# Queries by kv in one float32r pass a head, with the parts stacked in the rows, and statistics begun a chunk ahead

## The chip, the cores and the metric

The kernel runs on one core of one Trainium2 chip. The metric is the device time of one execution in microseconds. A core has TensorE (PE; its weight loads are listed as PEld), VectorE (DVE), ScalarE (ACT), GpSimd (POOL) and SyncE (SP), which here issues all DMAs. The engines work side by side, each through its own list of instructions in order, and wait for one another by semaphores.

## The reference

Linear attention over 8 batches, 8 heads, 576 tokens of 64 numbers, and behind it a gated feed-forward layer on the 4608 tokens of 512 numbers (`w_a` and `w_b` are 512 x 1536, `w_out` is 1536 x 512), all in float32:

```python
q_s = np.exp(q - max(q, axis=-1));  q_s = q_s / (sum(q_s, axis=-1) + 1e-09)
k_s = np.exp(k - max(k, axis=2));   k_s = k_s / (sum(k_s, axis=2) + 1e-09)
kv  = einsum('bhsd,bhse->bhde', k_s, v)
x   = einsum('bhsd,bhde->bhse', q_s, kv)      # 4608 x 512 after a transposition
a, b = x @ w_a, x @ w_b
out  = (a * b) @ w_out
```

## The kernel before, in words

**Number format.** A float32 number is kept as two float32r parts, hi and lo, and a product of two float32 matrices is three matmul passes: hi by hi, hi by lo, lo by hi. `split` makes the parts: a cast for hi (ACT, L341, or DVE), a subtraction for lo (DVE, L344).

**Chunks and loops.** The 4608 tokens are worked in nine chunks (0 to 8) of T = 512. The loop over `c` from 1 to 8 multiplies chunk `c` with both gate matrices, one of six pairs of 128 features of `w_a` and `w_b` after the other, and meanwhile prepares the attention result of chunk `c + 1`. A pair is computed by a scheme with seven products of half size instead of eight, from sums of blocks: `kx` = A11 B11, `ky` = S2 T2, `ka` = S3 T3, `kp` = S1 T1, then `kx` += A12 B21, `kp` += S4 B22 and `ka` += A22 T4. Each is 12 matmuls of 256 columns (`product`, L835) into one of three PSUM banks (k0 for `kx`, k1 for `ky` and then `kp`, k2 for `ka`), with weights `ws` that SP loads from DRAM (L475) and operands `xo` made of the chunk's `xf`. Between the products ACT copies `kx` to `u2` (L1443), DVE adds `ky`, `ka` and `kp` to it (L1444 to L1474), multiplies the halves and splits the gate's product to `gh` and `gl` (L341, L344). `run_pending` multiplies these by `w_out` into the four banks `po` (L864). So `kx` can be written a second time only when ACT has copied it, and `ky` of a pair only when DVE has read the `kp` that was in its bank.

**Preparing a chunk.** Three calls of `attend()` in each pair run a list of steps that `attention_tasks(c + 1)` has written, 18 calls in a loop. The steps for a batch that begins in the chunk are the softmax of k and kv = kT v for two heads at a time (`kv_two`, `pk`, L582), stored as a weight pair `kvh`, `kvl` of 128 x 128 with zeros outside the heads' own blocks. For the queries there are, for each of four head pairs `g`:

- `q_load` and `q_stats`: the queries by tokens; the negative maximum on DVE (L672), then eight exponentials of 128x64 on ACT with a summing output (L675), and small DVE operations. Behind the fourth pair `q_stats_out` transposes all statistics on TensorE (`pst`), copies them and writes them to DRAM as `dq` (L690).
- `q_rows`: four DMAs read `dq` back, spread over 64 rows each, as `mr` (L716: the negative maximum in `rows[0]`, the reciprocal sum in `rows[1]`); `q_turned`: the queries by features, `qtt`.
- `q_exp`: DVE adds `rows[0]`, ACT takes the exponential, `split` makes `qhl`.
- `x_product`: `px` = kv by q, three passes in the spare bank "at", in two pieces where a batch ends inside the chunk (L761); DVE multiplies by `rows[1]` into `xf` (L960).

**What sets the order.** The list of steps gives the call in which a step is issued. Tile's scheduler then orders each engine's instructions by its model of the times, buffers rotate through a few tiles each, and a table (`ORDER`) fixes the order of the first chunks' work. SP issues DMAs in that order, and one that waits holds up those behind it.

Of the kernel before, what the change touches and what calls it, by code (L numbers as in the profile page):

```python
# [255 lines left out]
def linear_attention_then_gated_ffn(  # L256
# [40 lines left out]
    TT = T // P  # L297
    NCH = NT // T
    LATE = NCH - qt_late.shape[0]

    const = ctx.enter_context(tc.tile_pool(name="const", bufs=1))
    sb = ctx.enter_context(tc.tile_pool(name="sb", bufs=2))
# [35 lines left out]
    def split(hi, lo, src, hi_engine="act"):  # L338

        if hi_engine == "act":  # L340
            nc.scalar.copy(out=hi, in_=src)  # L341
        else:
            nc.vector.tensor_copy(out=hi, in_=src)
        return nc.vector.tensor_tensor(out=lo, in0=src, in1=hi.bitcast(F32), op=ALU.subtract)  # L344
# [270 lines left out]
    def kv_two(b, g, kts, vts, tag):  # L615

        pk = ps.tile([P, 2, D + 1], F32, name="pk", tag=tag)
        for n in range(2):
            kv_sums(kts[n], vts[n], tag, pk[:, n])
        den = sb.tile([P, 2], F32, name="den2")  # L620
        nc.vector.tensor_scalar_add(den, pk[:, :, D], EPS)
        nc.vector.reciprocal(out=den, in_=den)
        kv = sb.tile([P, 2, P], F32, name="kv2", bufs=1)
# [6 lines left out]
        split(*kv_home(b, g), kv, "dve")  # L630


    wholes = sb.tile([P, 2, NP, P], F32, name="wholes", tag="mr", bufs=2)
# [5 lines left out]
    def kv_split_whole(b, g):  # L639
        kv_split(b, g, whole.pop((b, g)))  # L640
# [54 lines left out]
    def roomy(c):  # L695
        return c > LATE

# [23 lines left out]
    def q_exp(c, qt, rows):  # L721
        nc.vector.tensor_tensor(out=qt, in0=qt, in1=rows[0], op=ALU.add)
# [19 lines left out]
    def x_whole(c, g, qw, tag):  # L742

        t0 = c * T
        b0, b1 = t0 // S, (t0 + T - 1) // S
        n0 = min(T, (b0 + 1) * S - t0)
        px = ps.tile([P, T], F32, name="px", tag=tag)
        for b, s in ((b0, slice(0, n0)), (b1, slice(n0, T)))[:b1 - b0 + 1]:
            nc.tensor.matmul(px[:, s], whole[b, g], qw[:, s], start=True, stop=True)  # L749
        return px  # L750

    def x_product(c, g, qhl, tag="at"):
        qh, ql = qhl
# [161 lines left out]
                steps += [(), ()] * (g > 0) + [(s0, s1, s2)]  # L915
        return steps

    def attention_tasks(c):
# [12 lines left out]
        stats, last, turned, rows = [], [], [], []  # L931
        every = {}
        for g in range(NP):
            box = {}

            def a0(g=g, box=box):
                if g == 0:
                    every["st"] = sb.tile([P, NP, 2, 2, TT], F32, name="st", bufs=1)
                box["q"] = q_load(c, g)

            def a1(g=g, box=box):
                q_stats(box["q"], every["st"][:, g])
                if g == NP - 1:
                    every["dq"] = q_stats_out(c, every["st"])

            stats.append((a0, a1))
# [11 lines left out]
            def b2(g=g, box=box):  # L958
                px = x_product(c, g, box["e"])
                nc.vector.tensor_tensor(out=xfs[c][:, g], in0=px, in1=box["r"][1], op=ALU.mult)  # L960

            turned.append(t0)
            rows.append(r0)
            last.append((b1, b2) if roomy(c) else (lambda t0=t0, r0=r0: (t0(), r0()), b1, b2))
        stats, steps = pipeline(stats), pipeline(steps)
        seq = []
        for i in range(max(len(stats), len(steps))):
            seq.append((stats[i] if i < len(stats) else []) + (steps[i] if i < len(steps) else []))
        last = pipeline(last)
        if c > 3:  # L970
            begin = 3 * NI - 3 - len(last) - 2
# [419 lines left out]
    last = None  # L1391
    for c in range(1, NCH):
        more = c + 1 < NCH
        attend = Spread(attention_tasks(c + 1) if more else [], 3 * NI - 3 - (1 if c == 1 else 0))
        po = None
        x, xo = xo, {}
        pairs = list(range(NI))[::-1 if c % 2 else 1]
        for n, i in enumerate(pairs):
            def part(name):
                return named(f"{name}.{(c - 1) * NI + n}") if c < 5 else nullcontext()  # L1400
# [51 lines left out]
            if not end:  # L1452
                with part("proj"):
                    run_pending()
            with part("attend"):
                attend(c > 2 and last)
            kp = ps.tile([P, 2, H], F32, name="kp", tag="k1")
            multiply(kp, S1, T1, True)
            multiply(kx, A12, B21, False)
            with part("pair"):  # L1460
                nc.vector.tensor_tensor(out=cc[:, 3], in0=kp, in1=u3, op=ALU.add)  # L1461
                nc.scalar.copy(out=cc[:, 0, 0], in_=kx[:, 0])  # L1462
# [4 lines left out]
                    run_pending()  # L1467
            if po is None:
                po = [ps.tile([P, DM], F32, name=f"po{t}") for t in range(TT)]
            with part("attend"):  # L1470
                attend(c > 2 and last)
            multiply(kp, S4, B22, False)
# [65 lines left out]
```

## Time and profile before

| | us |
|---|---|
| median of 3 runs | 935.83 (935.6 to 938.75) |
| the profiled execution | 935.81 |
| its span | 934.0 |
| TensorE busy | 924.7 |
| VectorE busy | 618.0 |
| ScalarE busy | 394.0 |
| GpSimd busy | 107.9 |

The times come from one core; the profiled execution is one of the program's, recorded by the hardware profiler, and 1.81 us of it lie outside the span. Matmuls are pipelined: a group's busy time overlaps the next group's start, so what matmuls cost is read from one start to the next.

### The profile page before, as it was taken

The numbers are of one execution on the slowest core, as the hardware profiler recorded it, in microseconds if no ns is written. First come the engines' busy times: TensorE is split into PE (matmuls) and PEld (weight loads), VectorE is DVE, ScalarE is ACT, GpSimd is POOL, SyncE is SP. The second block draws the span as 40 slices with busy tenths as digits, with TensorE's granted clock in tenths as the row PEclk, the third lists the DMA queues.
The fourth block names the chain that finished last, engine by engine and source line by source line (L and its number), as shares of the span: only waits on it lengthen the run. The fifth ranks groups of instructions, "written<-read, shape, count | busy, mean of one in ns | idle before, by whom it ended". The sixth has DMA issues, their size and how long they took to land.

```text
span 934.0 us, 17535 instructions
## 1 busy us (share of the span) xinstructions
PE 924.7 (99%) x6565; PEld 835.2 (89%) x6565; DVE 618.0 (66%) x1218; ACT 394.0 (42%) x1094; POOL 107.9 (12%) x88
## 2 busy tenths in 40 slices
PE   8999999999999999999999999999999999999998
PEld 6677789999988999999999999999999999999997
DVE  7998898788854677467656574666657454753433
ACT  8988774435521345133613271324424352322111
POOL 1654434330000000000100010000000000000000
PEclk9999999999999999999999999999999999999999
DMA  9989889989788879983989289945997389627761
GB/s 349 349 308 367 333 321 337 330 310 285 266 305 291 259 270 345 283 330 110 337 255 380 94 302 297 361 169 198 331 320 247 102 293 308 219 96 270 248 224 47
DMA packets 88947, 253.27 MB, mean 271 GB/s; under 512 B 10720, under 2 KB 11296, under 8 KB 88864
## 3 DMA queue, kind: packets, MB, share of 16 engines
q1 hardware_dynamic: 88864, 252.16, 78.5%
q8 instruction: 52, 0.85, 0.4%
q14 instruction: 31, 0.25, 0.1%
HBM read 213.09 MB, written 36.93 MB: 268 GB/s over the span
## 4 chain that ended last, share of the span: by engine, by line
PE 95%; DVE 2%; DMA 1%; ACT 0%; POOL 0%; issue 0%; SPq 0%; DVEq 0%; POOLq 0%
PE po L864 31%; PE kx L835 14%; PE kp L835 14%; PE ka L835 14%; PE pt L805 7%; PE ky L835 7%; PE px L761 2%; PE pk L582 2%; PE po L850 1%; PE px L749 1%; DMA kt_first<-in_kt 1%; DVE xo L344 0%; POOL mx L512 0%; DVE kt L544 0%; DVE mc L1128 0%
## 5 line engine op out<-in xcount | busy, mean ns | idle before, releaser
L864 PE MATMUL po<-wo_w,gh 128*128 128x512 f32 x840 | 264.5, 396 | 0.0
L835 PE MATMUL kx<-xo,ws 128*128 128x256 f32 x1152 | 184.7, 282 | 0.3 <-DVE cc L1463 0.2
L835 PE MATMUL ka<-xo,ws 128*128 128x256 f32 x1152 | 177.7, 282 | 0.7 <-DVE u L1447 0.4
L835 PE MATMUL kp<-xo,ws 128*128 128x256 f32 x1152 | 174.8, 283 | 0.5 <-DVE cc L1461 0.5
L864 PEld LDWEIGHTS po<-wo_w,gh 128*128 128x128 f32 x840 | 151.3, 188 | 25.1 <-ACT gh L341 0.5
L835 PEld LDWEIGHTS kx<-xo,ws 128*128 128x128 f32 x1152 | 160.7, 189 | 6.7 <-DVE cc L1463 0.7
L835 PEld LDWEIGHTS ka<-xo,ws 128*128 128x128 f32 x1152 | 157.9, 189 | 6.7 <-issue 0.6
L835 PEld LDWEIGHTS kp<-xo,ws 128*128 128x128 f32 x1152 | 155.7, 189 | 5.8 <-DVE cc L1461 0.8
L864 PE MATMUL po<-wo_w,gl 128*128 128x512 f32 x420 | 153.0, 396 | 0.0
L341 ACT CAST gh<-cc 128x512 fp32r<-128x512 f32 x96 | 58.6, 620 | 168.8 <-DVE cc L1475 145.4
L1462 ACT COPY cc<-kx 128x256 f32<-128x256 f32 x48 | 17.8, 372 | 177.6 <-PE kx L835 170.4
L864 PEld LDWEIGHTS po<-wo_w,gl 128*128 128x128 f32 x420 | 78.0, 188 | 15.7 <-DVE gl L344 0.4
L1474 DVE TENSOR_TENSOR cc<-kp,u 128x512 f32<-128x512 f32 x48 | 33.1, 690 | 86.0 <-PE kp L835 85.9
L805 PE MATMUL pt<-xo,ws 128*128 128x512 f32 x288 | 87.0, 418 | 0.0
L835 PE MATMUL ky<-xo,ws 128*128 128x256 f32 x576 | 86.6, 281 | 0.0
L675 ACT ACTIVATE qt<-qt,st 128x64 f32<-128x64 f32 x224 | 75.3, 340 | 19.6 <-DVE st L672 18.7
L835 PEld LDWEIGHTS ky<-xo,ws 128*128 128x128 f32 x576 | 76.8, 189 | 1.1
L344 DVE TENSOR_TENSOR gl<-cc,gh 128x512 fp32r<-128x512 f32 x96 | 67.1, 704 | 12.9 <-ACT gh L341 12.8
L1461 DVE TENSOR_TENSOR cc<-kp,u 128x512 f32<-128x512 f32 x48 | 33.2, 691 | 62.7 <-PE kp L835 62.2
L805 PEld LDWEIGHTS pt<-xo,ws 128*128 128x128 f32 x288 | 52.9, 188 | 17.3 <-issue 4.2
L512 POOL PARTITION_ALL_REDUCE mx<-m x20 | 18.1, 910 | 433.0 <-DVE m L523 433.0
L1443 ACT COPY u<-kx 128x512 f32<-128x512 f32 x48 | 28.0, 583 | 51.5 <-PE kx L835 48.0
(150 smaller groups left out, 1117.3 us busy)
## 6 DMA issues: line engine op xcount, KB each, us to landing
ws<-dw SPq DMA_DIRECT2D x260, 512.0 KB, 6.0
dw<-ws SPq DMA_DIRECT2D x42, 512.0 KB, 6.6
mr<-dq SPq DMA_DIRECT2D x112, 128.0 KB, 6.0
raw<-in_w_ab SPq DMA_DIRECT2D x24, 512.0 KB, 7.8
out<-ot SPq DMA_DIRECT2D x36, 256.0 KB, 4.7
vt<-in_v SPq DMA_DIRECT2D x28, 325.0 KB, 6.1
qt<-in_q SPq DMA_DIRECT2D x32, 256.0 KB, 5.1
kt<-in_k SPq DMA_DIRECT2D x24, 320.0 KB, 5.3
```

Of the source, the lines that this page charges most:

```text
L341: nc.scalar.copy(out=hi, in_=src)
L344: return nc.vector.tensor_tensor(out=lo, in0=src, in1=hi.bitcast(F32), op=ALU.subtract)
L512: nc.gpsimd.partition_all_reduce(out_ap=mx, in_ap=kv_max(kt), channels=P, reduce_op=bass_isa.ReduceOp.max,)
L582: nc.tensor.matmul(pk[h * D:(h + 1) * D], kt[:, j, h], vt[:, j, h], start=(j == 0), stop=(j == J - 1),)
L675: nc.scalar.activation(out=qt[:, j, h], in_=qt[:, j, h], func=AF.Exp, bias=st[:, h, 0, j:j + 1], accum_out=st[:, h, 1, j:j + 1],)
L761: nc.tensor.matmul(px[:, s], w, m[:, s], start=(i == 0), stop=(i == 2))
L805: nc.tensor.matmul(pt, w[:, wp], x[g][:, xp], start=(g == 0 and i == 0), stop=(g == NP - 1 and i == 2),)
L835: ins = nc.tensor.matmul(pt[:, n], w[:, n, wp, c], x[:, xp, c], start=(first and n == 0 and i == 0), stop=(i == 5), skip_group_check=True,)
L864: ins = nc.tensor.matmul(po[t], a[:, ts], wo[f][:, w], start=(f == ends[0] and i == 0), stop=(f == ends[1] and i == 2),)
L1443: nc.scalar.copy(out=u2, in_=kx)
L1461: nc.vector.tensor_tensor(out=cc[:, 3], in0=kp, in1=u3, op=ALU.add)
L1474: nc.vector.tensor_tensor(out=cc[:, 1], in0=kp, in1=u2, op=ALU.add)
```

## The change

From chunk 5 on (`TALL = 5`, the sixth) a product of queries by kv is made head by head. The 64 rows of a head's queries that were in half of the rows of a tile are put there twice: the hi parts in the head's own half of one tile, the lo parts in the other half. The weight pair for a head has hi over hi in the columns of its own head, and lo over zeros in the other 64 columns. One pass of 128 rows then gives hi·hi + hi·lo in the head's own 64 output rows and lo·hi in the other 64. ACT copies the second half to the head's own rows of `rows[0]`, DVE adds the two halves, and one multiplication by `rows[1]` ends a head pair, as before. The two heads use two banks: "at", and whichever of k0 and k1 is free at this call. For it,

- `kv_tall` writes the weights of a batch with 64-row casts on DVE and ACT, a subtraction on DVE and a fill with zeros on POOL, and `kv_again` does it a second time for batch 4, on which chunk 5 begins;
- `q_exp` splits the two heads apart, with two casts and two subtractions of 64 rows;
- in loops with `c + 1 >= TALL` the product A12 B21 into `kx` is moved ahead of S1 T1 into `kp`, so that a bank is free;
- the queries' statistics of chunk `c + 2` are begun in loop `c`, for c = 3 to 6: loads at calls 11, 12, 16 and 17, the statistics of the first two head pairs at 12 and 14, of the other two at calls 0 and 1 of the next loop, and the rows, exponentials and products at fixed calls (products at 5, 7, 10 and 13; before at 10 to 14).

TensorE has 6166 matmuls in its list instead of 6194: 56 instead of 84 for `px` of chunks 5 to 8. DVE has 1282 instructions instead of 1220, ACT 888 instead of 824, POOL 110 instead of 94 and SP 672 DMAs as before.

```diff
+    def kv_tall(b, g, heads):
+        q = g // 2
+        w = [sb.tile([P, 2, P], F32R, name=f"kvt{x}{q}", tag=f"kv{x}{q}") for x in "hl"]
+        for n in (2 * q, 2 * q + 1):
+            kvs[b, n] = tuple(t[:, n % 2] for t in w)
+        for h, (hi, lo) in enumerate(heads):
+            me, it = own(h), own(1 - h)
+            nc.vector.tensor_copy(out=w[h][me, :, me], in_=hi)
+            nc.scalar.copy(out=w[h][it, :, me], in_=hi)
...
+            nc.gpsimd.memset(w[h][it, :, it].bitcast(F32), 0.0)
...
     def q_exp(c, qt, rows):
         nc.vector.tensor_tensor(out=qt, in0=qt, in1=rows[0], op=ALU.add)
         nc.scalar.activation(out=qt, in_=qt, func=AF.Exp)
+        if c >= TALL:
+            hl = sb.tile([P, 2, T], F32R, name="qhl", tag="mr", bufs=2)
+            for h in range(2):
+                split(hl[own(h), h], hl[own(1 - h), h], qt[own(h)])
+            return hl
...
+    def x_tall(c, g, hl, rows, xf):
...
+        for h, tag in enumerate((at["spare"], "at")):
+            px = ps.tile([P, T], F32, name=f"px{h}", tag=tag)
+            for s in (slice(0, edge), slice(edge, T))[:1 + (edge < T)]:
+                nc.tensor.matmul(
+                    px[:, s], kvs[(t0 + s.start) // S, g][h], hl[:, h, s], start=True, stop=True
+                )
+            me = own(h)
+            nc.scalar.copy(out=rows[0][me], in_=px[own(1 - h)])
+            nc.vector.tensor_tensor(out=xf[me], in0=px[me], in1=rows[0][me], op=ALU.add)
+        nc.vector.tensor_tensor(out=xf, in0=xf, in1=rows[1], op=ALU.mult)
...
+                for g, n in enumerate((5, 7, 10, 13)):
+                    exp, mul = every["last"][g]
+                    seq[max(n - 3, 3)] = seq[max(n - 3, 3)] + [rows[g], turned[g]]
+                    seq[n - 1] = seq[n - 1] + [exp]
+                    seq[n] = [mul] + seq[n]
...
+        if TALL <= c + 2 < NCH:
+            every, stats = stats_steps(c + 2)
+            todo, calls = todo + [[] for _ in range(len(todo), calls + 3)], calls + 3
+            for g, n in enumerate((11, 12, 16, 17)):
+                todo[n] = todo[n] + [stats[g][0]]
+            for g, n in enumerate((12, 14)):
+                todo[n] = todo[n] + [stats[g][1]]
+            ahead[c + 2] = every, [[s[1]] for s in stats[2:]]
...
+            if c + 1 >= TALL:
+                multiply(kx, A12, B21, False)
             kp = ps.tile([P, 2, H], F32, name="kp", tag="k1")
             multiply(kp, S1, T1, True)
-            multiply(kx, A12, B21, False)
+            if c + 1 < TALL:
+                multiply(kx, A12, B21, False)
```

How this moves instructions is shown at two places. The first is ScalarE in loop 6, in the fifth of the six pairs, where chunk 7 is prepared. A row has the line, the operation, what it writes and reads, and the size; `gh` is a gate's cast, `qtt` the exponential of the queries, `qhl` their hi part, `u` the copy of `kx`. Before:

```order
L723 ACTIVATE qtt<-qtt 128x512
L341 CAST qhl<-qtt 128x512
L341 CAST gh_8445<-cc 128x512
L341 CAST gh_8465<-cc 128x512
L1443 COPY u_8473<-kx 128x512
```

and now, where the rows of `qt,st` are the statistics of chunk 8:

```order
L342 CAST gh_8594<-cc 128x512
L758 ACTIVATE qtt<-qtt 128x512
L710 ACTIVATE qt,st<-qt,st 128x64
L342 CAST qhl<-qtt 64x512 x2
L710 ACTIVATE qt,st<-qt,st 128x64 x7
L1536 COPY u_8602<-kx 128x512
L342 CAST gh_8574<-cc 128x512
```

Eight instructions of the statistics and two casts of 64 rows have come between the exponential of the queries and the copy of `kx`. TensorE has in the same pair now:

```order
L890 MATMUL ka<-xo,ws 128x256 x3
L890 MATMUL kx<-xo,ws 128x256 x12
L890 MATMUL kp<-xo,ws 128x256 x12
L890 MATMUL ka<-xo,ws 128x256 x12
L890 MATMUL ky<-xo,ws 128x256 x12
L799 MATMUL px_8686<-qhl,kvtl_6992 128x448
L799 MATMUL px_8686<-qhl,kvtl_8198 128x64
L890 MATMUL kx<-xo,ws 128x256 x12
```

The first row ends the pair before. The second `kx` has moved ahead of `po` and `kp`, and one head's pass, in two pieces, stands right ahead of it.

The other place is the queue of SP, from the statistics' way to DRAM on: `dq` is written, and `mr` are the rows read back, `ws` weights, `kt` and `vt` the keys and values of a batch. Before, in loop 6:

```order
L690 DMA dq_7987<-sst 64x128
L475 DMA ws<-dw_740 128x1024
L475 DMA ws<-dw_856 128x1024
L716 DMA mr_8231<-dq_7987 64x512
L716 DMA mr_8232<-dq_7987 64x512
L716 DMA mr_8231<-dq_7987 64x512
L716 DMA mr_8232<-dq_7987 64x512
L716 DMA mr_8285<-dq_7987 64x512
```

and now:

```order
L725 DMA dq_7854<-sst 64x128
L476 DMA ws<-dw_621 128x1024
L476 DMA ws<-dw_586 128x1024
L751 DMA mr_8017<-dq_7854 64x512
L501 DMA kt<-in_k 128x640
L507 DMA vt<-in_v 128x650
L501 DMA kt<-in_k 128x640
L507 DMA vt<-in_v 128x650
L751 DMA mr_8018<-dq_7854 64x512
L751 DMA mr_8017<-dq_7854 64x512
L751 DMA mr_8018<-dq_7854 64x512
L751 DMA mr_8107<-dq_7854 64x512
```

Three more `mr` and two `ws` follow in both. The rows come at another time of the loop, and four loads of keys and values now lie between them, behind the one that waits for `dq`.

More of the change, by code (lines that the diff above doesn't have):

```diff
@@ L299, in linear_attention_then_gated_ffn @@
     LATE = NCH - qt_late.shape[0]
+    TALL = 5
     const = ctx.enter_context(tc.tile_pool(name="const", bufs=1))
@@ L622, in kv_two @@
         nc.vector.reciprocal(out=den, in_=den)
+        if b * S >= TALL * T:
+            kv = sb.tile([P, 2, P], F32, name="kv2", bufs=1)[:, :, 0:D]
+            nc.vector.tensor_tensor(
+                out=kv, in0=pk[:, :, 0:D], in1=den.unsqueeze(2).broadcast_to([P, 2, D]), op=ALU.mult,
+            )
+            kv_tall(b, g, [(kv[own(h)], None) for h in range(2)])
+            return
         kv = sb.tile([P, 2, P], F32, name="kv2", bufs=1)
@@ L630, in kv_two, with own, kv_again @@
         split(*kv_home(b, g), kv, "dve")
+    def own(h):
+        return slice(h * D, (h + 1) * D)
+    def kv_tall(b, g, heads):
[7 more added lines that the diff above has]
+            nc.scalar.copy(out=w[h][it, :, me], in_=hi)
+            if lo is None:
+                nc.vector.tensor_tensor(
+                    out=w[h][me, :, it], in0=hi, in1=w[h][me, :, me].bitcast(F32), op=ALU.subtract
+                )
+            else:
+                nc.vector.tensor_copy(out=w[h][me, :, it], in_=lo)
+            nc.gpsimd.memset(w[h][it, :, it].bitcast(F32), 0.0)
+    def kv_again(b):
+        for g in range(0, NP, 2):
+            kvh, kvl = kv_parts[b, g // 2]
+            kv_tall(b, g, [[x.bitcast(F32)[own(h), :, own(h)] for x in (kvh, kvl)] for h in range(2)])
     wholes = sb.tile([P, 2, NP, P], F32, name="wholes", tag="mr", bufs=2)
@@ L916, in key_steps, with stats_steps, a0, a1 @@
         return steps
+    ahead = {}
+    def stats_steps(c):
+        every, stats = {}, []
+        for g in range(NP):
+            box = {}
+            def a0(g=g, box=box):
+                if g == 0:
+                    every["st"] = sb.tile([P, NP, 2, 2, TT], F32, name="st", bufs=1)
+                box["q"] = q_load(c, g)
+            def a1(g=g, box=box):
+                q_stats(box["q"], every["st"][:, g])
+                if g == NP - 1:
+                    every["dq"] = q_stats_out(c, every["st"])
+            stats.append((a0, a1))
+        return every, stats
     def attention_tasks(c):
@@ L930, in attention_tasks @@
                 ))
-        stats, last, turned, rows = [], [], [], []
-        every = {}
-        for g in range(NP):
[L934 to L946, printed above, removed]
+        if c == TALL and c * T % S:
+            steps = [(lambda: kv_again(c * T // S),)] + steps
+        last, turned, rows = [], [], []
+        if c in ahead:
+            every, stats = ahead[c][0], []
+        else:
+            every, stats = stats_steps(c)
+        for g in range(NP):
             box = {}
@@ L958, in b2 @@
             def b2(g=g, box=box):
+                if c >= TALL:
+                    x_tall(c, g, box["e"], box["r"], xfs[c][:, g])
+                    return
                 px = x_product(c, g, box["e"])
@@ L968, in attention_tasks @@
             seq.append((stats[i] if i < len(stats) else []) + (steps[i] if i < len(steps) else []))
+        every["last"] = last
         last = pipeline(last)
         if c > 3:
+            if c >= TALL:
+                seq = [[] for _ in range(3 * NI - 3)]
+                for n, now in enumerate(ahead[c][1]):
+                    seq[n] = seq[n] + now
+                for n, now in enumerate(steps):
+                    seq[n] = seq[n] + now
+                for g, n in enumerate((5, 7, 10, 13)):
[3 more added lines that the diff above has]
+                    seq[n] = [mul] + seq[n]
+                return seq
             begin = 3 * NI - 3 - len(last) - 2
@@ L1393, in linear_attention_then_gated_ffn @@
         more = c + 1 < NCH
-        attend = Spread(attention_tasks(c + 1) if more else [], 3 * NI - 3 - (1 if c == 1 else 0))
+        todo, calls = attention_tasks(c + 1) if more else [], 3 * NI - 3 - (1 if c == 1 else 0)
+        if TALL <= c + 2 < NCH:
[6 more added lines that the diff above has]
+            ahead[c + 2] = every, [[s[1]] for s in stats[2:]]
+        attend = Spread(todo, calls)
         po = None
@@ L1469, in linear_attention_then_gated_ffn @@
                 po = [ps.tile([P, DM], F32, name=f"po{t}") for t in range(TT)]
+            at["spare"] = "k0"
             with part("attend"):
```

4 lines of the change are left out of this document (added).

## The prediction, made before the changed kernel was run

> **What bounds the kernel now.** I read the page first: the profiled execution took 935.81 us, 934.0 of them span, so 1.81 us lie around the span, and the sum below is made against 935.81. The median shown, 935.83, is the same within 0.02.
>
> ```profile
> span 934.0 us, 17535 instructions
> PE 924.7 (99%) x6565; PEld 835.2 (89%) x6565; DVE 618.0 (66%) x1218; ACT 394.0 (42%) x1094; POOL 107.9 (12%) x88
> PE 95%; DVE 2%; DMA 1%; ACT 0%; POOL 0%; issue 0%; SPq 0%; DVEq 0%; POOLq 0%
> ```
>
> TensorE is busy 99% of the span and 95% of the chain that ended last. That is an average, so I cut the time by stages next. A row of the windows view has the stretch and its length, then busy time (and instructions) of PE, PE's weight loads, DVE, ACT and POOL, the granted clock, the DMA share and GB/s.
>
> ```profile
> 300.00:500.00 200.00, 200.00 (x1512) 185.28 (x1511) 128.80 (x261) 73.17 (x222) 7.52 (x8) 1.00 0.83 276
> 700.00:900.00 200.00, 200.00 (x1384) 186.04 (x1383) 106.45 (x194) 56.37 (x149) 0.00 (x0) 1.00 0.67 223
> ```
>
> From 300 to 900 us, where all that is changed takes place (the first TensorE instruction that differs stands at about 380 us), TensorE never waits: 200.00 of 200.00 us at clock 1.00. So here a matmul less is time won at once, and any wait that TensorE gets is time lost at once. In the first of the two stretches DVE is busy 128.80/200 = 64%, ACT 37%, the DMA 83%: room on average, which does not say that they are never late.
>
> **What the change takes away.** In the products of queries by kv of chunks 5 to 8, three passes become two of the same width, one a head. The timeline of TensorE shows one product of each of the four chunks. Where the product lies between others, its cost is from its start to the next row's start.
>
> ```profile
> 501.92 0.46 PE L761 MATMUL px<-qhl,kvh 128*128 128x320 f32 x2
> 502.22 0.31 PE L761 MATMUL px<-qhl,kvl 128*128 128x320 f32 x1
> ...
> 502.68 0.54 PE L835 MATMUL kx<-xo,ws 128*128 128x256 f32 x3
> ```
>
> ```profile
> 597.46 0.52 PE L761 MATMUL px<-qhl,kvh 128*128 128x384 f32 x2
> ...
> 598.27 1.64 PE L835 MATMUL kp<-xo,ws 128*128 128x256 f32 x12
> ```
>
> ```profile
> 697.04 0.56 PE L761 MATMUL px<-qhl,kvh 128*128 128x448 f32 x2
> ...
> 697.89 1.68 PE L835 MATMUL kp<-xo,ws 128*128 128x256 f32 x12
> 699.41 0.76 PE L835 MATMUL ka<-xo,ws 128*128 128x256 f32 x5
> ```
>
> ```profile
> 798.02 0.62 PE L761 MATMUL px<-qhl,kvh 128*128 128x512 f32 x2
> 798.48 0.39 PE L761 MATMUL px<-qhl,kvl 128*128 128x512 f32 x1
> 798.71 1.23 PE L835 MATMUL kx<-xo,ws 128*128 128x256 f32 x9
> ```
>
> Chunk 5: 0.76 us, chunk 6: 0.81, chunk 7: 0.85, chunk 8: 0.69. A third of each is 0.25, 0.27, 0.28 and 0.23. With four head pairs a chunk that is 4 x 1.03 = 4.1 us, and 16 products in all. Nothing else leaves TensorE: **-4.1 us**, certain up to 0.3 for the short passes. As there was no wait to remove, it is also all that can be won.
>
> **What it adds off TensorE.** A head pair now takes one split more on DVE and on ACT (two of 64 rows instead of one of 128), two adds of 64 rows on DVE and two copies of 64 rows on ACT. The width of 512 sets the time of such an instruction here, not its rows, or so I take it; rows for DVE, ACT and the statistics:
>
> ```profile
> 702.59 0.69 DVE L722 TENSOR_TENSOR qtt<-qtt,mr 128x512 f32<-128x512 f32 x1
> 703.19 0.68 DVE L960 TENSOR_TENSOR xf<-px,mr 128x512 f32<-128x512 f32 x1
> 703.79 0.68 DVE L344 TENSOR_TENSOR gl<-cc,gh 128x512 fp32r<-128x512 f32 x1
> ```
>
> ```profile
> 653.53 0.59 ACT L1443 COPY u<-kx 128x512 f32<-128x512 f32 x1 [2.60 <-PE kx L835]
> 654.01 1.14 ACT L341 CAST gh<-cc 128x512 fp32r<-128x512 f32 x2
> 655.05 0.35 ACT L675 ACTIVATE qt<-qt,st 128x64 f32<-128x64 f32 x1
> ...
> 657.38 0.33 ACT L675 ACTIVATE qt<-qt,st 128x64 f32<-128x64 f32 x1
> ```
>
> DVE's step is 0.60 back to back, ACT's 0.52 (two casts in 655.05 - 654.01 = 1.04). Three more on each, 16 times: 16 x 1.8 = 29 us of DVE and 16 x 1.56 = 25 us of ACT, some 7 and 6 us in each chunk of about 100. The idle third of DVE and the idle two thirds of ACT hide that on average. What counts is where they stand ahead of something that TensorE waits for. The eight exponentials of a pair's statistics take 8 steps of (657.38 - 655.05)/7 = 0.333, that is 2.67 us of ACT in one piece. They are not new, but they move.
>
> **Place one: the second kx behind the statistics.** The change puts the second kx product ahead of kp, and pieces of statistics into the fourth to sixth pair of a loop. In the order shown above for the fifth pair, ACT has gh, the exponential, one statistic, two 64-row casts, seven statistics and only then the copy u of kx, without which TensorE cannot write kx again. TensorE has ahead of that: kx, kp, ka, ky, one head's px. A product takes 699.41 - 697.89 = 1.52 with the lead of a weight load behind px, and 1.42 between others:
>
> ```profile
> 620.77 1.59 PE L835 MATMUL ky<-xo,ws 128*128 128x256 f32 x12
> 622.19 1.60 PE L835 MATMUL ka<-xo,ws 128*128 128x256 f32 x12
> ```
>
> So it arrives 4 x 1.42 + 0.29 (half of chunk 7's 0.85 x 2/3) = 5.97 us after it left the old ka. For ACT, count from that same moment:
>
> ```profile
> 699.61 0.69 DVE L1474 TENSOR_TENSOR cc<-kp,u 128x512 f32<-128x512 f32 x1 [0.82 <-PE kp L835]
> 700.33 0.42 DVE L1475 TENSOR_TENSOR cc<-cc 128x256 f32<-128x256 f32 x1
> ```
>
> ```profile
> 700.79 0.62 ACT L341 CAST gh<-cc 128x512 fp32r<-128x512 f32 x1 [4.34 <-DVE cc L1475]
> ```
>
> A gate's cast starts 700.79 - 699.41 = 1.38 after its product ended. DVE goes on at about 1.34 with the add of q (0.60) and the statistics' maximum, ready at 1.34 + 0.60 + 0.68 = 2.62:
>
> ```profile
> L672 DVE TENSOR_REDUCE st<-qt 128x8 f32<-128x512 f32 x28 | 19.0, 679 | 2.0 <-DMA qt<-in_q 2.0
> ```
>
> ACT's cast is over by 1.90, and its exponential, which waits for the add of q (2.02), by about 2.02 + 0.52 = 2.5. Then 2.67 of statistics, 1.04 of casts, 0.59 of copy: 2.62 + 2.67 + 1.04 + 0.59 = 6.92. TensorE stands still for 6.92 - 5.97 = 0.95 us. The move of kx is made in loops 4 to 7 and statistics ahead in loops 3 to 6, so both meet in three loops: **+2.9 us** (0 if the maximum comes 0.95 us earlier; twice it if DVE is as late again).
>
> **Place two, the last pair of the same three loops.** The copy u comes 0.2 + 0.52 (a cast) + 2.67 + 0.52 (gh) + 0.59 = 4.50 after kx ended, TensorE gets there after kp, ka and ky, 3 x 1.42 = 4.26: 0.24 a loop, **+0.7 us**.
>
> **ky behind DVE.** ky takes the bank in which kp lies until DVE has added u to it, and DVE has more of 64 rows ahead of such an add. No trace shows that wait. Between nothing and one DVE step of 0.69 I take half, 0.35, in one pair of each of four loops: **+1.4 us** (0 to 2.8).
>
> **The queue of SP.** The q rows (mr) of a chunk and the loads of q and of k and v now stand at other calls, and weights (ws) queue behind them in order.
>
> ```profile
> 666.40 0.47 SPq L690 DMA_DIRECT2D dq<-sst  x1
> 667.40 0.80 SPq L475 DMA_DIRECT2D ws<-dw  x2
> 669.10 4.92 SPq L716 DMA_DIRECT2D mr<-dq  x8
> ```
>
> ```profile
> ws<-dw SPq DMA_DIRECT2D x260, 512.0 KB, 6.0
> raw<-in_w_ab SPq DMA_DIRECT2D x24, 512.0 KB, 7.8
> ```
>
> One mr holds SP 4.92/8 = 0.615 us, a ws 0.40. The first mr must wait until dq has landed: 669.10 - 666.40 = 2.7 us. In the new order of loop 6 (quoted above), what lies between the statistics' transposition and the second ws behind the rows is: about 1.2 until dq can be issued (an estimate, two DVE steps), 2.7, eight mr 4.9, four loads of k and v 1.6, two ws 0.8, that is 11.2 us; and 6.0 to land makes 17.2. TensorE has 100 matmuls of 256 columns (100 x 1.42/12 = 11.8), 24 of 512 (24 x (798.48 - 798.02)/2 = 5.5) and some 1.5 us of small ones ahead of the ka that takes these weights: 18.8. It holds by 1.6 us at the median landing, and a landing as of raw's 7.8 uses that up. I take **+0.3** in all, with 0 and 6.3 (2.1 in each of three loops, for a landing of 9.7) as ends.
>
> What else is new costs nothing while TensorE is busy: 16 small zero fills on POOL, idle there (0.00 to 7.52 us of 200), and the four batch-4 rebuilds on DVE and ACT in one loop, which lie before chunk 5's first product by several calls.
>
> The sum: 935.8 - 4.1 + 2.9 + 0.7 + 1.4 + 0.3 = **937.0 us**. A measurement of this kernel can tell about 0.5%, 4.7 us, from no change: below 931.1 is faster, above 940.5 slower.
>
> **A rule that speaks against it.** The rows at 702.59 to 703.79 show DVE starting each instruction 0.08 us before the one ahead of it is over (0.60 against 0.68), all of them on 128 rows. On those rows the sum stands. The Trainium skill, "VectorE: DVE Perf Modes", section "Two Vector instructions with no wait between them", says that an instruction whose input or output starts in another group of 32 partitions than the last access of that memory is held until every earlier one has finished. No run here shows it on this path, and no DVE instruction of the products of before begins at row 64.
>
> **The rivals.** *Clean gain.* If DVE's maximum comes a step earlier, the copy u is early at both places and only the 4.1 us are seen, less up to 2: 931.7 to 933.5. For it: ACT is idle 63% of the time. Against it: the order puts the copy behind all eight statistics. 0.16.
>
> *Weights late behind the rows: slower.* Its place is the ka of the second pair in loops 4 to 6, its price 2.1 us each, and it decides from a landing of 7.6 us on. For it: the DMA is busy 67 to 83% in these stretches, and other 512 KB loads took 7.8 at the median. Against it: ws itself took 6.0, and so far TensorE waited for none. 935.8 - 4.1 + 5.0 + 6.3 = 943.0 us. 0.19.
>
> *DVE loses its overlap where it changes halves.* The two subtractions, the two adds and the multiplication behind them change halves; 5 x 0.08 = 0.4 us of DVE in each of 16, and where ky waits for DVE, four times, the price is 1.6 us: 938.6 us, inside my own case and not slower by the bound. By the rule of the Trainium skill just named this would be what happens. 0.05.
>
> *The passes do not shrink* cannot be: the order counts 6166 TensorE matmuls for 6194, and no new shapes.
>
> **Chances.** Forecast 0.57 (933.5 to 940.5), clean 0.16, weights 0.19, halves 0.05, and a gain beyond all that I count 0.03. So faster 0.03, same 0.57 + 0.16 + 0.05 = 0.78, slower 0.19. The range from 931.7 to 942.0 takes in the clean case and the forecast with its ends, and leaves out most of the slower one.
>
> **What would show it.** TensorE's busy time of the px groups falls by 28 instructions and about 4 us. Its waits, none after 300 us before, should show kx released by ACT's u (about 1 us, in three loops, fifth pair), ky by DVE's cc, and ka by ws hardly at all. If no kx waits for u, place one is wrong; if ws waits add up to more than 3 us, the weights rival is right; if the time is under 931, TensorE had a wait that I did not see.

## The result, and the profile of the changed kernel

The changed kernel took 949.13 us (median of 6 runs, 947.82 to 956.11) against 936.69 us (median of 6): a ratio of the means of 1.0142, with a 95% interval of 1.0110 to 1.0173. It is slower by 1.4%, and outside the range of 931.7 to 942.0. Its profiled execution took 949.01 us with 947.2 us of span, 13.2 us more than that of before. Ratios and intervals here and below leave out executions in a slow state, of which there was one, of 5142 us, in the kernel under "Both later". The first lines of the changed kernel's page:

```profile
span 947.2 us, 17583 instructions
PE 927.5 (98%) x6537; PEld 833.9 (88%) x6537; DVE 652.2 (69%) x1280; ACT 430.2 (45%) x1158; POOL 111.1 (12%) x104
PE 84%; DVE 6%; DMA 4%; ACT 3%; issue 1%; SPq 1%; POOL 0%; DVEq 0%; POOLq 0%
```

VectorE has 34 us more work and ScalarE 36, where 29 and 25 had been worked out for the products alone. But the chain that ended last, 95% TensorE before, is now 84% TensorE, and 13% VectorE, DMA and ScalarE. The windows say where: the two stretches that held 200.00 us of TensorE before hold less.

```profile
300.00:500.00 200.00, 195.39 (x1481) 180.87 (x1480) 137.88 (x283) 83.36 (x242) 9.28 (x18) 1.00 0.84 283
700.00:900.00 200.00, 197.85 (x1359) 182.80 (x1358) 113.68 (x204) 65.28 (x163) 0.00 (x0) 1.00 0.64 222
```

The view of waits, for TensorE from 300 us on, was empty before. Now it has 17 waits, 10.7 us (total, times, longest):

```profile
PE kx L890 <- ACT u L1536: 4.1, 6, 1.1
PE kx L890 <- DVE xf L804: 2.2, 1, 2.2
PE ka L890 <- DMA ws<-dw: 2.1, 2, 1.8
PE px L799 <- DVE qhl L345: 1.0, 4, 0.3
PE ky L890 <- DVE cc L1572: 1.0, 3, 0.5
PE kp L890 <- DVE cc L1558: 0.3, 1, 0.3
```

**Place one** can be read off the timelines of the fifth pair of loop 6, first TensorE, then ScalarE. The column behind the start is the group's duration, and the bracket has the idle time and what ended it.

```profile
716.14 1.65 PE L890 MATMUL ky<-xo,ws 128*128 128x256 f32 x12
718.03 0.50 PE L799 MATMUL px<-qhl,kvtl 128*128 128x448 f32 x2 [0.25 <-DVE qhl L345]
719.63 1.71 PE L890 MATMUL kx<-xo,ws 128*128 128x256 f32 x12 [1.10 <-ACT u L1536]
721.18 0.62 PE L919 MATMUL po<-wo_w,gh 128*128 128x512 f32 x2
```

```profile
714.92 0.35 ACT L710 ACTIVATE qt<-qt,st 128x64 f32<-128x64 f32 x1
715.26 1.25 ACT L342 CAST qhl<-qtt 64x512 fp32r<-64x512 f32 x2
716.54 0.35 ACT L710 ACTIVATE qt<-qt,st 128x64 f32<-128x64 f32 x1
...
718.54 0.33 ACT L710 ACTIVATE qt<-qt,st 128x64 f32<-128x64 f32 x1
718.99 0.59 ACT L1536 COPY u<-kx 128x512 f32<-128x512 f32 x1
```

Eight statistics and two casts, then the copy u, which ends at 719.58; kx starts at 719.63. That is the wait as it was worked out, in kind. Its size, 1.10 for 0.95, came out so near partly by luck, because both sides were late: the copy u ended 7.70 us after the first kx of the pair began (at 711.88), where 6.92 had been worked out, and TensorE, which px had held up, was ready for kx at 718.37 (719.63 less 1.10 and the 0.16 explained below), 6.49 after it, where 5.97 had been.

The rows also show a second thing: a wait costs more than its bracket. Had nothing been late, ky would have taken 1.42 us and px 0.28, and kx would have begun at 717.84. It began at 719.63, 1.79 us later, and the brackets hold 0.25 + 1.10 = 1.35 of that. And kx itself took 721.18 - 719.63 = 1.55 instead of 1.42. Two waits have cost 1.92 us, about 0.28 each beyond the idle time shown. The same holds at the other waits: by the pitch of the matmuls ahead of it, each start is 0.16 us later than its bracket says, and the first matmuls behind it lose about another 0.10. The 0.16 are how the profile models the end of a matmul: it lets one of 256 columns last 0.28 us, while the next begins 0.12 us after its start.

**A chain that I had not seen** ends in the longest wait, in loop 4, where chunk 5 is prepared. This is the chain of work from 450 to 473 us (start, duration, what):

```profile
450.64 4.45 DMA dq<-sst
455.11 0.45 SPq L751
...
456.25 6.22 DMA mr<-dq
...
462.59 0.70 DVE qtt L757
...
463.32 0.64 ACT qtt L758
...
464.64 0.69 DVE qhl L345
...
467.56 0.35 DVE m L522
...
469.64 0.69 DVE xf L804
...
471.23 0.69 DVE xf L804
...
471.96 1.09 PE kx L890 x7
```

The statistics go to DRAM (4.45 us; before the change it was 2.28 for the same statistics), the q rows come back (6.22), the queries are added, raised and split, and then VectorE takes the softmax of a batch's keys (from L522 on) before it reads px. That px lies in bank k0, which the next pair's kx needs: TensorE stands for 2.25 us (2.2 in the view of waits). Before the change nothing but the pairs' own products used that bank in this loop.

### The profile page after: what moved, and what is told of

Its sections match the earlier page's. It is cut to its first block, busy times and chain, and to the rows that moved or that the text cites. A ratio compares the mean times of both kernels' runs of the same rounds, so it can differ in the third digit from the quotient of the medians.

```text
span 947.2 us, 17583 instructions
## 1 busy us (share of the span) xinstructions
PE 927.5 (98%) x6537; PEld 833.9 (88%) x6537; DVE 652.2 (69%) x1280; ACT 430.2 (45%) x1158; POOL 111.1 (12%) x104
## 4 chain that ended last, share of the span: by engine, by line
PE 84%; DVE 6%; DMA 4%; ACT 3%; issue 1%; SPq 1%; POOL 0%; DVEq 0%; POOLq 0%
PE po L919 28%; PE kx L890 13%; PE ka L890 12%; PE kp L890 12%; PE pt L860 7%; PE ky L890 6%; DMA mr<-dq 2%; PE pk L583 2%; DMA ws<-dw 2%; ACT qt L710 2%; PE po L905 1%; PE px L816 1%; PE warm L332 1%; PE px L789 1%; PE px L799 1%
## 5 line engine op out<-in xcount | busy, mean ns | idle before, releaser
L890 PE MATMUL kx<-xo,ws 128*128 128x256 f32 x1152 | 182.4, 283 | 6.6 <-ACT u L1536 4.1
L890 PE MATMUL kp<-xo,ws 128*128 128x256 f32 x1152 | 172.9, 282 | 0.8 <-DVE cc L1558 0.8
L919 PE MATMUL po<-wo_w,gl 128*128 128x512 f32 x420 | 150.7, 397 | 0.0
L345 DVE TENSOR_TENSOR gl<-cc,gh 128x512 fp32r<-128x512 f32 x96 | 66.9, 702 | 14.2 <-ACT gh L342 13.2
```

The lines of the kernel that those rows point to most:

```text
L890: ins = nc.tensor.matmul(pt[:, n], w[:, n, wp, c], x[:, xp, c], start=(first and n == 0 and i == 0), stop=(i == 5), skip_group_check=True,)
L919: ins = nc.tensor.matmul(po[t], a[:, ts], wo[f][:, w], start=(f == ends[0] and i == 0), stop=(f == ends[1] and i == 2),)
```

## The experiments

My theory after the result: the passes are won, and what is lost is waits made by the order, above all the statistics a chunk ahead and the early products. Rivals: the one-pass products are too dear for VectorE, ScalarE and the banks wherever they stand; or SP's queue. Before ran beside each kernel, and each ratio is to the before of its own group: 936.27 us beside the statistics in their own loop, ahead alone, the statistics at other calls and one chunk later; 936.72 beside both later, kp ahead of kx, the join left out and the add on GpSimd; 936.87 beside the other four. An edit is shown against the changed kernel unless something else is said.

### Statistics in their own loop

```diff
-                for n, now in enumerate(ahead[c][1]):
+                for n, now in enumerate(stats):
...
-                for g, n in enumerate((5, 7, 10, 13)):
+                for g, n in enumerate((10, 11, 13, 14)):
...
-        if TALL <= c + 2 < NCH:
+        if False:
```

> The changed kernel with the statistics of the queries put back into their own loop (calls 0 to 4, as before) and the products at calls 10, 11, 13 and 14. One pass a head, the new weights and the kx product ahead of kp stay. My theory (what was lost is waits, and most of them come from beginning the statistics a chunk ahead: exponentials ahead of the copy u, and products so early that q rows must come right behind the statistics): the waits for u (4.1 us) and for xf (2.2 us) go, the 3 to 4 us of passes stay won, 933 to 935 us. Rival one (the one-pass products themselves are too dear for VectorE and ScalarE, or hold the banks too long): most of the loss stays, 944 to 949 us. Rival two (the queue of SP): weights come as before, about 945 us from 949 us, since only the 2.1 us of waits for ws and their consequences go.

Measured: 936.98 us, ratio 1.0006 (0.9996 to 1.0015). 12 us of the loss are gone, and with them every wait for u, xf and ws. So the calls at which the steps stand were the cause of the loss, and the first rival falls as an account of it. But the gain of 3 to 4 us that I expected is not there either. Four waits of ky for VectorE are left, 1.4 us:

```profile
PE ky L890 <- DVE cc L1572: 1.4, 4, 0.9
```

### Ahead alone, with the three passes of before

```diff
-                if c >= TALL:
+                if False:
                     x_tall(c, g, box["e"], box["r"], xfs[c][:, g])
...
-            if c + 1 >= TALL:
+            if False:
                 multiply(kx, A12, B21, False)
```

and in the same manner in `q_exp`, `kv_two` and ahead of `kv_again`.

> The changed kernel with the three passes of before on the old weights and with kp ahead of kx again; statistics begun a chunk ahead and the calls of rows, exponentials and products as in the change. My theory: without kx moved ahead the copy u has one product more of time (1.42 us against 1.1 us of wait), and no px lies in the bank of kx, so that only late q rows of the first of the loops could hold TensorE: 936 to 939 us. Rival one (the products are what costs): 936 to 937 us, no different from before. Rival two (the queue of SP): the order of SP's transfers is that of the change, so waits for ws of 2 us or more remain, 940 to 945 us.

Measured: 938.34 us, ratio 1.0022 (1.0012 to 1.0031), as my theory had it: slower by about 2 us, with five small waits (0.6 for ws, 0.7 for qhl, 0.2 for cc). Beginning the statistics a chunk ahead and placing products early costs something even without the new products. The large waits need the rest of the change as well; whether it is the one-pass products or the move of kx that they need, this run does not show, since it takes back both.

### Statistics at other calls

```diff
-            for g, n in enumerate((12, 14)):
+            for g, n in enumerate((13, 16)):
```

> The changed kernel with the first two pairs' statistics of the next chunk at calls 13 and 16 instead of 12 and 14, so that their exponentials are issued behind the copy u of their pair and not ahead of it. My theory: the wait of kx for u (4.1 us in six waits) goes to under 1 us, and each wait gone gives back about 0.25 us more than its idle time; 944 to 946 us, with the waits for xf, ws and qhl left. Rival one (products too dear): u is late because of the products' casts and copies, the waits stay, 948 to 950 us. Rival two (queue of SP): 949 us, as the waits for u are not its matter.

Measured: 940.92 us, ratio 1.0055 (1.0034 to 1.0076): two numbers give back 8 us of the 12. The waits for u are gone, as place one says, and more than I expected went with them:

```profile
PE ky L890 <- DVE cc L1572: 2.6, 4, 0.8
PE px L799 <- DVE qhl L345: 0.9, 3, 0.3
PE ka L890 <- DMA ws<-dw: 0.4, 1, 0.4
```

The 2.2 us of kx for xf in loop 4 is missing too. There VectorE's add of the q rows began at 460.91 us instead of 462.59 (though the statistics took longer to land, 6.11 us), its two adds of px ran in one piece instead of around a subtraction for the keys, and 20 matmuls of keys by values stood ahead of kx. The products were as early as in the changed kernel, so that wait hangs on a margin of a microsecond or two; which of these shifts removed it was not tried.

### One chunk later

```diff
-    TALL = 5
+    TALL = 6
```

> The changed kernel with TALL = 6, so that chunk 5 is computed as before and the new form begins at chunk 6, one loop later. My theory: if the 7 us lost in loop 4 come from the first use of the form (weights rebuilt, statistics and rows of the loop before not ahead), they move to loop 5 and the time hardly changes, 945 to 949 us; if they come from what else loop 4 does (its own place among weights and keys), they go, and the time is 941 to 943 us. Rival two (queue of SP): the load of the queue is alike in loops 4 to 6, each loop costs the same, and the time is about 946 us.

Measured: 944.38 us, ratio 1.0078 (1.0047 to 1.0109). It lies below the range for "moved to the next loop" and above that for "gone", near the rival's 946. In the trace a part did move: kx for xf is now 0.8 us, in loop 5, with new waits of 1.0 for kp and 0.8 for ka; u's are 2.8 in four. The run does not tell the theories apart.

### Products at later calls

```diff
-                for g, n in enumerate((5, 7, 10, 13)):
+                for g, n in enumerate((10, 11, 13, 14)):
```

> The changed kernel with the products at calls 10, 11, 13 and 14 instead of 5, 7, 10 and 13, statistics still begun at calls 12 and 14 of the loop before. With the runs that moved the statistics alone (940.9 us) and both (939.5 us) it makes a square. My theory: the waits of kx for u in the fifth and sixth pair stay or grow, since eight exponentials and now a product's split and copies meet there; the waits for xf and the pressed q rows go; 944 to 948 us. Rival (the early products and their q rows are the main cause, the statistics only add to it): 939 to 941 us.

Measured: 946.61 us, ratio 1.0106 (1.0078 to 1.0133): in the range that I gave, by another mechanism. The waits for u are gone, which I had expected to stay. Instead weights are late:

```profile
PE ka L890 <- DMA ws<-dw: 5.5, 4, 2.3
PE ky L890 <- DVE cc L1572: 1.8, 7, 0.4
PE px L799 <- DVE qhl L345: 0.6, 3, 0.2
```

This is the rival that I had priced at 2.1 us a loop: here two of the waits are 2.23 and 2.34, in loops 5 and 6, with the rows of the chunk spread over SP's list right ahead of those weights. In the changed kernel it stayed at 2.1 us in all.

These two waits cost more again. 0.1 us after TensorE had gone on behind the first, and 1.4 us behind the second, the clock that it was granted fell to 0.50 for 3.4 us. The windows show it (the clock is the third number from the end, and a mean over the stretch):

```profile
587.60:591.20 3.60, 3.60 (x18) 3.60 (x19) 0.00 (x0) 0.00 (x0) 0.00 (x0) 0.53 1.02 407
693.40:697.00 3.60, 3.60 (x20) 3.60 (x19) 0.78 (x2) 0.00 (x0) 0.00 (x0) 0.53 1.03 418
```

From the end of each wait on, 24 and 36 matmuls of 256 columns took some 1.5 us more than at the usual pitch. It does not follow every wait of this length: behind the 2.25 us of the changed kernel the clock stayed at 1.00. The mean clock of this profiled execution is 0.996 and its time 948.60 us. Of the other three, 943.81 and 944.62 us have a clock of 1.000 and 950.39 us one of 0.995, so the median of 946.61 lies between two groups.

### Both later

```diff
-                for g, n in enumerate((5, 7, 10, 13)):
+                for g, n in enumerate((10, 11, 13, 14)):
...
-            for g, n in enumerate((12, 14)):
+            for g, n in enumerate((13, 16)):
```

> The changed kernel with statistics begun a chunk ahead at calls 13 and 16, and with the products at calls 10, 11, 13 and 14 instead of 5, 7, 10 and 13. My theory: with the exponentials behind u and the q rows no longer pressed, waits of px for qhl, kx for xf and ka for ws are gone, and what remains is VectorE's, as with statistics in their own loop; 935 to 938 us. Rival (beginning statistics ahead costs in itself, through SP's queue, as the 2.1 us of the run with three passes could mean): 938 to 941 us, with waits for ws or qhl.

Measured: 939.45 us, ratio 1.0030 (1.0019 to 1.0041). It is the rival's: waits for ws (2.0 in two) remain, one of ky behind the add of the q rows (1.1), and VectorE's four of ky for cc (1.4), as with statistics in their own loop. With the products at the same calls, statistics in their own loop take 937.0 and statistics ahead 939.5, so at these calls being ahead costs some 2.5 us. The square is: 949.1 as changed, 946.6 with late products, 940.9 with later statistics, 939.5 with both. By these medians the calls of the statistics are worth 7 to 8 us, those of the products 1.4 to 2.5. The corner with late products is the weak one: from its two executions at clock 1.000 the statistics would be worth about 5 there and the products about 5. The 8 us of the statistics' calls with early products do not hang on it.

### The move of kx alone, and without it

The kernel before with kx ahead of kp in loops 4 to 8:

```diff
-            multiply(kp, S1, T1, True)
+            if c < 4:
+                multiply(kp, S1, T1, True)
             multiply(kx, A12, B21, False)
+            if c >= 4:
+                multiply(kp, S1, T1, True)
```

> The kernel before, with the second kx product ahead of kp in loops 4 to 8 and nothing else changed. My theory: TensorE has no waits before and the copy u still comes in time without statistics ahead of it; 936 to 937 us, no difference. Rival (the move alone makes kx wait for u, since ScalarE has one product less of time): waits of kx for u of 1 us or more in sum, 938 us or more.

Measured: 936.94 us, ratio 1.0001 (0.9991 to 1.0010), no waits. The move alone is free. The other way round, the statistics in their own loop and kp ahead of kx:

> The statistics in their own loop, and the second kx product behind kp again, as before the change. One head's product then uses the bank that kp needs next. My theory: at the two products of a loop that use that bank kp now waits for VectorE's add, about 1 us each when nothing else stands between, or the scheduler puts other work there; 938 to 943 us with waits of kp for xf. Rival (the move of kx is what loses the rest of the gain): 934 to 936 us.

Measured: 938.16 us, ratio 1.0025 (1.0013 to 1.0038), against 1.0006 with kx first. No kp waited for xf; the scheduler put other work between, and the waits are of ky for cc (1.9), ka for ws (1.7) and once kx for u (0.3). The time was in my range and the mechanism was not.

### Who makes ky wait

With the statistics in their own loop, four waits of ky were left. The joining of the halves was my first suspect. This kernel leaves out the lo by hi part of the product (this edit and the next three are shown against the kernel with the statistics in their own loop):

```diff
-            nc.scalar.copy(out=rows[0][me], in_=px[own(1 - h)])
-            nc.vector.tensor_tensor(out=xf[me], in0=px[me], in1=rows[0][me], op=ALU.add)
-        nc.vector.tensor_tensor(out=xf, in0=xf, in1=rows[1], op=ALU.mult)
+            nc.vector.tensor_tensor(out=xf[me], in0=px[me], in1=rows[1][me], op=ALU.mult)
```

> The statistics in their own loop, as in the run of that kind, and the joining of the two halves left out: ScalarE's two copies and VectorE's two adds of 64 rows for each product are gone, and two multiplications of 64 rows by the rows remain instead of one of 128 (so the lo by hi part of the product is missing from the output). My theory: the four waits of ky for VectorE (1.4 us of idle, about 2.4 us with what a restart costs) are made by these instructions, and go; 934.0 to 935.0 us, against 937.0 with the join and 936.3 before. Rival (the rest of the gain is lost on TensorE itself, in eight insertions a loop instead of four): no change, 936.5 to 937.5 us.

Measured: 938.48 us, ratio 1.0016 (1.0008 to 1.0025), a miss: no faster than with the join (1.0006, and the intervals overlap), and the four waits of ky are 2.8 us. Ahead of the add that ky waits for there now stood another 128-row instruction, an operand of the next chunk. The second attempt moved another instruction off VectorE:

```diff
-        nc.vector.tensor_tensor(out=qt, in0=qt, in1=rows[0], op=ALU.add)
+        (nc.gpsimd if c >= TALL else nc.vector).tensor_tensor(out=qt, in0=qt, in1=rows[0], op=ALU.add)
```

> The statistics in their own loop, and the add of the q rows to the queries moved from VectorE to GpSimd for chunks 5 to 8 (16 instructions of 128x512); output as the reference's. My theory: VectorE gets back 0.6 us ahead of each product, the waits of ky for it (0.89 us the longest) shrink below 0.3 in sum, and the one-pass products win at last, 934.5 to 935.8 us, a little under before. Rival one (insertions on TensorE): 936.5 to 937.5 us. Rival two (the add on GpSimd is so much slower that the exponentials and products come late): waits of px for qhl appear, 938 us or more.

Measured: 939.93 us, ratio 1.0033 (1.0021 to 1.0045), a miss as well: the time is rival two's, but the waits of px for qhl that were to show it are not there. The same add of 128x512 takes 1.36 us on GpSimd for VectorE's 0.69, the exponentials come later, and there are ten waits, 3.8 us, eight of them of ky and kp for VectorE's cc (2.7) (the row's columns are busy time, mean ns, idle before):

```profile
L757 POOL TENSOR_TENSOR qtt<-qtt,mr 128x512 f32<-128x512 f32 x16 | 21.8, 1362 | 166.1 <-DMA mr<-dq 129.5 <-DMA qtt<-in_q_late 27.9 <-DMA ws<-dw 8.1
```

So less work was not the point. VectorE's own list at the longest of these waits, in the run with statistics in their own loop, shows what is:

```profile
701.68 1.40 DVE L804 TENSOR_TENSOR xf<-px,mr 64x512 f32<-64x512 f32 x2
703.12 1.41 DVE L345 TENSOR_TENSOR qhl<-qtt,qhl 64x512 fp32r<-64x512 f32 x2
704.55 0.69 DVE L805 TENSOR_TENSOR xf<-xf,mr 128x512 f32<-128x512 f32 x1
705.28 0.69 DVE L1572 TENSOR_TENSOR cc<-kp,u 128x512 f32<-128x512 f32 x1
```

TensorE's timeline at the same place:

```profile
703.30 1.59 PE L890 MATMUL kx<-xo,ws 128*128 128x256 f32 x12
704.72 0.42 PE L799 MATMUL px<-qhl,kvtl 128*128 128x448 f32 x2
706.02 1.68 PE L890 MATMUL ky<-xo,ws 128*128 128x256 f32 x12 [0.89 <-DVE cc L1572]
```

The matmuls of kp had all been started by 703.30, where kx begins. The add that frees its bank stood behind a pair of 64-row instructions and a multiplication that nobody waits for so soon. It was enough to put that multiplication behind the add:

```diff
-        nc.vector.tensor_tensor(out=xf, in0=xf, in1=rows[1], op=ALU.mult)
+        deferred.append(lambda: nc.vector.tensor_tensor(out=xf, in0=xf, in1=rows[1], op=ALU.mult))
...
-                nc.vector.tensor_tensor(out=cc[:, 1], in0=kp, in1=u2, op=ALU.add)
+                added = nc.vector.tensor_tensor(out=cc[:, 1], in0=kp, in1=u2, op=ALU.add)
+                with tc.issue_after(added.ins):
+                    while deferred:
+                        deferred.pop(0)()
```

> The statistics in their own loop, and each product's last multiplication (VectorE, 128x512) put behind the add of u to kp that frees ky's bank; output as the reference's. My theory (the waits of ky come from where VectorE's instructions stand in its list, with pairs of 64-row instructions taking 1.40 to 1.43 us where 128-row ones would take 1.20): the waits of ky, 1.4 us in four, fall to under 0.3, and each wait gone gives back its idle time and some 0.25 us; 934.5 to 935.5 us, 1 us or more under before. Rival (what is left of the gain is lost on TensorE, at eight insertions a loop, whatever VectorE does): 936 to 937 us though the waits are gone.

Measured: 934.84 us, ratio 0.9982 (0.9973 to 0.9991): faster than both kernels, by 2 us against before. The same place now:

```profile
703.75 0.69 DVE L1572 TENSOR_TENSOR cc<-kp,u 128x512 f32<-128x512 f32 x1
704.36 1.28 DVE L805 TENSOR_TENSOR xf<-xf,mr 128x512 f32<-128x512 f32 x2
```

```profile
704.50 1.68 PE L890 MATMUL ky<-xo,ws 128*128 128x256 f32 x12 [0.16 <-DVE cc L1572]
```

The waits of ky are 0.6 us in four, where I had said under 0.3; the time is as expected. The same work in another order on one engine is worth some 2 us here.

### The passes without their price

This kernel leaves out the arrangement of the parts and the second head; VectorE and ScalarE do what they did before.

```diff
-            for h in range(2):
-                split(hl[own(h), h], hl[own(1 - h), h], qt[own(h)])
+            split(hl[:, 0], hl[:, 1], qt)
...
-            nc.scalar.copy(out=rows[0][me], in_=px[own(1 - h)])
-            nc.vector.tensor_tensor(out=xf[me], in0=px[me], in1=rows[0][me], op=ALU.add)
-        nc.vector.tensor_tensor(out=xf, in0=xf, in1=rows[1], op=ALU.mult)
+        nc.vector.tensor_tensor(out=xf, in0=px, in1=rows[1], op=ALU.mult)
```

> The statistics in their own loop, and VectorE and ScalarE left with as much for a product as before: one split of 128 rows, no copies and adds, one multiplication of 128 rows that reads the first head's bank (so neither the arrangement of the parts nor the second head reaches the output). TensorE's passes and their order rules are those of the change. My theory: this is the change without its price, no waits, before less 3 to 4 us, 932.5 to 934 us. Rival (lost on TensorE): 935.5 to 937 us without waits.

Measured: 935.37 us, ratio 0.9987 (0.9978 to 0.9996). My 932.5 to 934 was missed; by the time it is nearly the rival's, but not without waits. The view of waits has one, and TensorE's timeline around it shows how much it hides:

```profile
798.52 1.59 PE L887 MATMUL ka<-xo,ws 128*128 128x256 f32 x12
800.36 1.70 PE L887 MATMUL ky<-xo,ws 128*128 128x256 f32 x12 [0.26 <-DVE cc L1569]
801.90 0.87 PE L887 MATMUL kx<-xo,ws 128*128 128x256 f32 x6
```

ka would have ended at 798.52 + 1.42 = 799.94, so ky is 0.42 late, and it takes 1.54 instead of 1.42: 0.54 us lost for a bracket of 0.26. By the same reckoning seven more late starts of ky in loops 4 to 7, with 0.13 us of idle time in all, cost between 0.1 and 0.4 us each, so that 2.0 us go there. VectorE's add to kp is late for ky even with the work of before. At all eight places the kx product that used to stand between kp and ky has been put ahead of kp, so that one product and not two gives VectorE its time. The move of the second kx alone does not do that: in the kernel with that move and nothing else, kx stands between as before, and no ky is late. A run with this one order put back was not made. The `px` groups, beside which this kernel has no wait, win some 4.7 us (12.5 before, 7.7 here, from each start to the next group's start), of which 1.5 are seen in the medians; so some 1.2 us stay open.

## Why the prediction was wrong, step by step

| step | predicted, us | in the changed kernel, us |
|---|---|---|
| third pass gone, 16 products | -4.1 | -4.7 |
| place one, kx for u, fifth pair | +2.9 | 0.92 + 1.10 + 1.10 = +3.1 |
| place two, kx for u, last pair | +0.7 | 0.35 + 0.29 + 0.34 = +1.0 |
| ky behind VectorE | +1.4 | +1.0 |
| SP's queue, ka for ws | +0.3 | +2.1 |
| kx for xf, px for qhl, kp for cc | none | 2.2 + 1.0 + 0.3 = +3.5 |
| what a wait costs beyond its idle time | none | 17 x 0.26 = +4.4 |
| sum | +1.2 | +10.4 of 13.2 |

The px groups of chunks 5 to 8, from each start to the next group's start less idle time, took 12.5 us before and 9.1 now. But 1.3 of the 9.1 are what waits in front of px and behind it cost beyond their idle time, which the last row counts; without them 7.8 are left, as in the kernel of the passes without their price, where it is 7.7. Of the 2.8 us that the sum lacks, 0.7 stand before 342 us already, where both kernels run the same list; the rest is open.

**The steps that held.** The passes are worth a third of the old products and a little more, 4.7 for 4.1, outside the 0.3 that the forecast allowed itself. Place one was right in its place and its loops, as the rows at 716 to 721 us and the move of the statistics to calls 13 and 16 show, and its size came out near, by the luck told above; place two, 1.0 for 0.7, and ky, 1.0 for 1.4, were near too. Width and not rows set the time of such an instruction here: the 64x512 adds of VectorE take 0.69 us each, as 128x512 ones did.

**The step that failed** is the sum over "place one, place two, ky behind VectorE, the queue of SP" as the full list of new waits, each priced at its idle time. First, the list was short. I followed each bank only to the engine that had read it before; that px now lies in the banks of kx and kp, and that VectorE must read it there behind whatever its list holds, was missing. So was a head's pass, which waits for a 64-row subtraction (four waits of 0.2 to 0.3, three of them of the second head). Second, the price was short: 0.26 us more for each of 17 waits is 4.4 us, about as much as the passes win. Third, the SP term was sized at 0.3 between ends of 0 and 6.3; it measured 2.1, most of it a single 1.81 in loop 4. The slower rival, weights two microseconds late in each of three loops, is not what happened here, though the run with late products, with such waits in two loops, shows that it can.

**The rule on halves.** The forecast took 0.60 us for VectorE's step whatever the rows. The pairs above that change halves take 1.40 and 1.41 us, so their second instruction starts about 0.72 after the first, when the first is over, and the next step follows 1.43 to 1.44 after the pair began. Changing halves thus costs 0.12 us for each instruction, not the 0.08 of the forecast's rival. The Trainium skill, "VectorE: DVE Perf Modes", section "Two Vector instructions with no wait between them", says that such an instruction starts only when every earlier one has finished; the trace agrees. The rival built on it, 1.6 us where ky waits for VectorE, was right in kind. All the waits of ky for VectorE are 1.0 us of idle time here, so it was not the cause of the 12 us.

**The clean gain**, 2.3 to 4.1 us in the forecast, was not reached: the best order tried brings 2.0 us, with four short waits left that cost 4 x (0.16 + 0.26) = 1.7.

## What to carry to other kernels

On an engine that never waits, list for each thing that is moved or added every buffer and bank that it now holds and who needs that next, and give each new wait a price above its idle time. Where a step can be put at one of many calls, the call can be worth more than the step: here two numbers were worth 8 us and the position of one multiplication 2 us, against the 4 to 5 us that the whole change could win. Between instructions that nobody awaits soon and one that frees a bank, state the order instead of leaving it to the scheduler.

## What the runs showed of the hardware that was not expected

- A wait of TensorE costs more than the idle time that the profile gives it: 0.42 us late with 0.26 of idle time shown, 0.16 less at every wait looked at, and a product of twelve matmuls behind a wait takes 1.50 to 1.55 us instead of 1.42. A start that is less than 0.16 us late shows no idle time at all.
- Behind two waits of TensorE of 2.23 and 2.34 us the granted clock read 0.50 for 3.4 us, which cost some 1.5 us each; behind one of 2.25 us in another run it stayed at 1.00.
- Two 64-row instructions of VectorE in a row that change halves take 1.40 us, two of 128 rows 1.28.
- The 32 KB of statistics took 3.7 to 4.5 us to land in loops 3 to 7, where they had taken 1.8 to 3.1 before.
